# Sixteen short loads on SyncE and 64 semaphore increments on TensorE in an attention kernel

## The chip, the cores and the metric

The kernel runs on one core of a Trainium2 chip. The metric is the device time of one execution in microseconds (us); the time before is the median of three runs, 634.53 us (634.51 to 634.56). A core has five engines with programs of their own: TensorE (PE, matmuls), VectorE (DVE), ScalarE (ACT), GpSimd (POOL) and SyncE (SP, which here issues loads). They meet through semaphores. Transfers run on 16 DMA engines, which take their work from queues.

## The reference

Attention without a mask, for 8 x 16 = 128 heads, 16 queries and 2048 keys of 256 elements a head, in bf16:

```python
B, H, Sq, Skv, Dh = 8, 16, 16, 2048, 256

def reference(q, k, v):
    scale = q.shape[-1] ** -0.5
    scores = jnp.einsum('bhqd,bhkd->bhqk', q, k) * scale
    attn = _softmax(scores, axis=-1)
    return jnp.einsum('bhqk,bhkd->bhqd', attn, v)
```

K and V are 134 MB each; all of both has to be read once.

## The kernel before

**Tiling.** The 128 heads are worked in G = 16 blocks of 8 heads; 8 heads x 16 queries fill the 128 partitions. A block's K is 8 MB, loaded in two halves of 4 MB (`load_k`, e = 0 and 1), its V is 8 MB. `SL` is the buffer for all of it: four slots of 4 MB, two for V (VA, VB) and two for K (KA, KB). There is one buffer for the K and one for the V of a block, so a load waits until TensorE has read what stood there. Block 0's K goes through the V slots.

**Stages of a block.** VectorE transposes K in place in 32 x 32 blocks (`kt`, L196, four for a block). TensorE makes the scores (`qk`, 64 matmuls into `S_ps`, lines L309 and L310). VectorE takes the maximum (L220), ScalarE the exponential (L292), VectorE transposes the result (L229, L231), and VectorE and ScalarE copy it into the sparse weights `PTz` (L203, L205, L277). TensorE multiplies with V (`pv`, L332, 128 matmuls with a weight load each into `O_ps`), ScalarE scales the output into `O_fin` (L271) and issues the store (L301).

**TensorE's program** (`on_tensor`). It waits for the first query weights (`c_qw`, L337), clears the score banks with four matmuls, computes the scores of block 0 in small loops, and enters the main loop over r = 1 to 16: scores of block r (up to 15), 20 matmuls into `X_ps` that nothing reads in most rounds, then PV of block r - 1. The loop is rolled: each round runs the same instructions, some 64 score matmuls and 128 PV matmuls with their weight loads.

**SP's program** (`on_sync`). It issues every load on one queue (q1 in the profile), in program order, and each load waits for the semaphore that says its slot is free: `c_qk` counts finished score halves, `c_pv` finished sixteenths of PV. After the start, a loop over j = 2 to 14 issues the two halves of K of block j (L146, L127) and then V of block j - 1 (L147, L132, L133). The last K comes in quarters, the last two blocks of V in 3 and 9 pieces (`PIECES`), each with a semaphore of its own, so that PV can start on what has landed. At the end SP waits for the last eviction (`c_ev`, L155), issues the last store (L156) and waits for it.

**GpSimd's program** (`on_gpsimd`) begins with 17 semaphore increments (L163), which set starting counts.

Of the kernel before, what the change touches and what calls it, by code (L numbers as in the profile page):

```python
# [11 lines left out]
BF16 = mybir.dt.bfloat16  # L12
# [8 lines left out]
def bass_standalone__softmax_full_bidir__sampling_kernel(  # L21
# [16 lines left out]
    ku = k.rearrange("b h s d -> (b h s) d").rearrange("(u p t) d -> u p t d", p=128, t=T)  # L38
# [4 lines left out]
    with ExitStack() as es:  # L43
        ec = es.enter_context
# [9 lines left out]
        PTz = ec(nc.sbuf_tensor("PTz", [128, 2, T, 128], BF16))  # L54
        mk = ec(nc.sbuf_tensor("mk", [128, 1], F32))
        O_fin = ec(nc.sbuf_tensor("O_fin", [128, D], BF16))
        negm = ec(nc.sbuf_tensor("negm", [128, 1], F32))
        lsum = ec(nc.sbuf_tensor("lsum", [128, 2], F32))
        ltot = ec(nc.sbuf_tensor("ltot", [128, 1], F32))
# [6 lines left out]
        def sem(name):  # L66
            return ec(nc.semaphore(name))
# [6 lines left out]
        s_v0 = sem("s_v0")  # L74
        s_st = sem("s_st")
        s_fin = sem("s_fin")
        c_pool = sem("c_pool")
        c_qt = sem("c_qt")
        c_cq = sem("c_cq")
# [46 lines left out]
        def load_k(eng, g, e, slot, t0, n, s):  # L126
            eng.dma_start(SL[:, slot, t0:t0 + n, :], ku[2 * g + e, :, t0:t0 + n, :]).then_inc(s, 16)  # L127

        def on_sync(eng):
            def load_v(w, a, n):  # L130

                eng.wait_ge(c_pv, 8 * w + (a + n + C - 1) // C)  # L132
                eng.dma_start(VW[:, a:a + n, :], vb[w, :, a:a + n, :]).then_inc(s_p[w][a] if a else s_v, 16)  # L133

            eng.dma_start(QX, qh).then_inc(s_q, 16)  # L135
            for g, s0, s in ((0, VA, s_k0), (1, KA, s_k)):
                for e in range(2):
                    load_k(eng, g, e, s0 + e, 0, T, s[e])

            for e in range(2):  # L140
                eng.wait_ge(c_qk, 4 * e + 4)
                eng.dma_start(VW[:, T * e:T * e + T, :], vb[0, :, T * e:T * e + T, :]).then_inc(s_v0 if e else s_v, 16)
            with nc.Fori(2, last, engines=[SP]) as j:
                for e in range(2):
                    eng.wait_ge(c_qk, 8 * j + 4 * e - 4)
                    load_k(eng, j, e, KA + e, 0, T, s_k[e])  # L146
                load_v(j - 1, 0, 2 * T)  # L147
            for e in range(2):
                eng.wait_ge(c_qk, 8 * last + 4 * e - 4)
                load_k(eng, last, e, KA + e, 0, T // 2, s_k[e])  # L150
                load_k(eng, last, e, KA + e, T // 2, T // 2, s_kl[e])
            for w in PIECES:
                for a, n in PIECES[w]:
                    load_v(w, a, n)
            eng.wait_ge(c_ev, G + 1)  # L155
            eng.dma_start(oh[last], O_fin[:]).then_inc(s_fin, 16)  # L156
            eng.wait_ge(s_fin, 16)

# [146 lines left out]
        def on_tensor(eng):  # L305
            def mm(dst, w, x, start, stop, load, check=True):

                if load:
                    return eng.matmul(dst, w, x, start=start, stop=stop, skip_group_check=not check)  # L309
                return eng.add_instruction(mybir.InstMatmult(  # L310
                    name=nc.get_next_instruction_name(), engine=PE, start_tensor_calc=start, stop_tensor_calc=stop,
                    bass_skip_group_check=not check, ldweights=False, tile_size=(128, 128), tile_position=(0, 0),
                    ins=[eng.lower_ap(x), eng.lower_ap(w, for_matmul_weights=True)], outs=[eng.lower_ap(dst)]))

            def qk(e, cs, slot):
                for bp in range(8):
                    for c in cs:
                        ins = mm(S_ps[:, c, :], QW[:, e, :, bp], SLk[:, slot, c, bp // 2, bp % 2, :, :],
                                 e == 0 and bp == 0, e == 1 and bp == 7, c == cs[0])
                return ins  # L320

            def pv(lim):

                for t in range(2 * T):
                    if t == T:
                        eng.wait_ge(s_v0, 16)
                        eng.wait_ge(c_cp, 10 * r + 1)
                        eng.wait_ge(c_cd, 6 * r)
                    for w in s_p:
                        if t in s_p[w]:  # L330
                            eng.wait_ge(s_p[w][t], lim[w])
                    ins = eng.matmul(O_ps[:, 0:D], PTz[:, t // T, t % T, :], VW[:, t, :],  # L332
                                     start=(t == 0), stop=(t == 2 * T - 1))
                    if t % C == C - 1:
                        ins.then_inc(c_pv, 1)

            eng.wait_ge(c_qw, 4)  # L337

            for c in range(4):
                if c == 0:  # L340
                    eng.wait_ge(c_pool, 1)
                mm(S_ps[:, c, :], PTz[:, 0, 0, :], PTz[:, 0, 0:4, :].rearrange("p t m -> p (t m)"), True, False, c == 0, False)
            with nc.Fori(0, 2, engines=[PE]) as e:
                for h in range(2):
                    with nc.Fori(0, 4, engines=[PE]) as b:
                        eng.wait_ge(c_kt, 2 * e + h + 1)
                        for par in range(2):
                            for c in (2 * h, 2 * h + 1):
                                ins = mm(S_ps[:, c, :], QW[:, e, :, 2 * b + par], SLk[:, VA + e, c, b, par, :, :],
                                         False, False, c == 2 * h, False)  # L350
                        if h:
                            ins.then_inc(c_qk, 1)

            with nc.Fori(1, G + 1, engines=[PE]) as r:
                rr = eng.to_reg(r)
                with eng.If_lt(rr, G):
                    for e in range(2):
                        for h in range(2):
                            eng.wait_ge(c_kt, 4 * r + 2 * e + h + 1)
                            if e + h == 0:  # L360
                                eng.wait_ge(c_ex[1], rr)
                            ins = qk(e, (2 * h, 2 * h + 1), KA + e)
                        ins.then_inc(c_qk, 4)

                    mid = eng.to_reg(((r + 14) & 16) + ((r + 1) & 16))
                    with eng.If_eq(mid, 16):
                        with nc.Fori(0, SPARE, engines=[PE]) as x:
                            for _ in range(4):
                                mm(X_ps[:], QW[:, 1, :, 7], QT[:, 0:512], True, True, False)
                lim = {last - 1: eng.to_reg(((r + 1) & 16) + 1), last: eng.to_reg((r & 16) + 1)}  # L370
                eng.wait_ge(c_ev, rr)
                eng.wait_ge(c_cp, 10 * r - 5)
                eng.wait_ge(c_cd, 6 * r - 2)
                eng.wait_ge(s_v, 16 * r)
                pv(lim)

        on_sync(nc.sync)
        on_gpsimd(nc.gpsimd)
        on_vector(nc.vector)
        on_scalar(nc.scalar)  # L380
        on_tensor(nc.tensor)


# [26 lines left out]
```

## Time and profile before

| | us |
|---|---|
| median of three runs (lowest, highest) | 634.53 (634.51, 634.56) |
| the profiled execution | 634.58 |
| its span in the profile | 633.3 |
| TensorE matmul busy | 539.7 (85%) |
| VectorE busy | 444.2 (70%) |
| ScalarE busy | 241.8 (38%) |
| moved by DMA | 270.56 MB, 427 GB/s over the span |

The profile is of one execution. Its page gives busy times of engines and queues, a chain of work that ended last (followed back from the last instruction, at each step to what released it), and groups of instructions by source line. Names such as SPq or PEldq stand for an engine's own sequencer: register steps, semaphores, issuing of transfers. A DMA queue's row has its packets, MB, and the time of its packets as a share of 16 engines' time in the window. Instruction queues (q8, q14) carry blocks of the engines' programs. A share can come out a little over 1, since a packet is counted where it starts.

### The profile page before, as it was taken

How to read it: one execution, taken by the hardware profiler on the slowest of the kernel's cores; microseconds unless marked ns; L12 is line 12 of the kernel's file. 1: busy time of each engine (PE TensorE's matmuls, PEld its weight loads, DVE VectorE, ACT ScalarE, POOL GpSimd, SP SyncE). 2: the span in 40 equal slices, each digit the busy share in tenths (PEclk: the TensorE clock that was granted, in tenths of full speed). 3: DMA queues.
4: the chain of work that ended last, by engine and by line, in shares of the span. 5: the costliest groups of instructions: out<-in, count | busy, mean ns of one | idle time of the engine just before them, and what ended most of it. 6: DMA issues, size and time to landing. Idle time of an engine off the chain costs nothing.

```text
span 633.3 us, 8100 instructions
## 1 busy us (share of the span) xinstructions
PE 539.7 (85%) x3336; PEld 272.9 (43%) x2561; DVE 444.2 (70%) x285; ACT 241.8 (38%) x309; POOL 21.5 (3%) x18
## 2 busy tenths in 40 slices
PE   1659989889898897989979899797989979899998
PEld 0112824518244282542725336263362724518386
DVE  5989794765948658496575965759567595769750
ACT  1026542623326233352424425244252442623453
POOL 7600000000000000000000000000000000000000
PEclk9998989999898999989999899999998999999999
DMA  8999999999999999999999999999999999999997
GB/s 364 443 447 433 428 464 401 450 409 431 441 422 442 423 433 458 407 457 408 455 417 421 447 423 441 446 410 457 408 456 417 423 441 424 439 418 430 430 426 299
DMA packets 11234, 270.56 MB, mean 427 GB/s; under 512 B 1248, under 2 KB 3424, under 8 KB 3936
## 3 DMA queue, kind: packets, MB, share of 16 engines
q1 hardware_dynamic: 9072, 269.55, 98.8%
q10 hardware_dynamic: 2160, 0.98, 0.5%
q8 instruction: 1, 0.02, 0.0%
q14 instruction: 1, 0.01, 0.0%
HBM read 269.48 MB, written 1.05 MB: 427 GB/s over the span
## 4 chain that ended last, share of the span: by engine, by line
DMA 57%; PE 34%; DVE 5%; issue 3%; SPq 0%; DVEq 0%; ACT 0%
DMA SL<-in_v_dram 49%; PE O_ps L332 32%; DMA SL<-in_k_dram 8%; DVE SL L196 4%; PE S_ps L309 1%; PE S_ps L310 1%; DVE PTb L231 0%; DVE negm L220 0%; DVE PTa L229 0%; DVE PTz L203 0%; DVE PTz L205 0%; SPq L133 0%; SPq L127 0%; ACT O_fin L271 0%; SPq L135 0%
## 5 line engine op out<-in xcount | busy, mean ns | idle before, releaser
L196 DVE STREAM_TRANSPOSE SL<-SL 128x4096 f32<-128x4096 f32 x64 | 282.4, 4433 | 82.0 <-DMA SL<-in_k_dram 81.2
L309 PE MATMUL S_ps<-SL,QW 128*128 128x512 bf16 (+1 forms) x512 | 206.5, 403 | 68.9 <-DVE SL L196 59.1
L332 PEld LDWEIGHTS O_ps<-SL,PTz 128*128 128x128 bf16 x2048 | 198.6, 98 | 103.1 <-DMA SL<-in_v_dram 79.3
L332 PE MATMUL O_ps<-SL,PTz 128*128 128x256 bf16 x2048 | 227.2, 273 | 12.9 <-DMA SL<-in_v_dram 11.5
L310 PE MATMUL S_ps<-SL,QW 128*128 128x512 bf16 (+1 forms) x512 | 204.8, 400 | 0.0
L309 PEld LDWEIGHTS S_ps<-SL,QW 128*128 128x128 bf16 (+1 forms) x512 | 74.3, 145 | 245.1 <-issue 155.3
L263 ACT ACTIVATE QW<-QT 32x256 bf16 x64 | 26.9, 420 | 203.0 <-PE S_ps L310 201.8
L277 ACT ACTIVATE PTz<-PTa 16x1024 bf16<-16x1024 bf16 x32 | 33.8, 1056 | 111.8 <-PE O_ps L332 100.0
L220 DVE TENSOR_REDUCE negm<-S_ps 128x1 f32<-128x2048 f32 x16 | 36.6, 2289 | 55.1 <-PE S_ps L310 55.1
L310 PE MATMUL X_ps<-QT,QW 128*128 128x512 bf16 x260 | 58.2, 379 | 0.0
L277 ACT ACTIVATE PTz<-PTb 16x1024 bf16<-16x1024 bf16 x48 | 50.6, 1055 | 10.9 <-ACT O_fin L271 10.1
L229 DVE STREAM_TRANSPOSE PTa<-P_sb 128x1024 bf16<-128x1024 bf16 x32 | 39.2, 1224 | 21.9 <-ACT P_sb L292 21.9
L277 ACT ACTIVATE PTz<-PTa,mk 32x1024 bf16<-32x1024 bf16 x48 | 54.3, 1130 | 0.0
L231 DVE STREAM_TRANSPOSE PTb<-P_sb 128x1024 bf16<-128x1024 bf16 (+1 forms) x32 | 39.0, 1219 | 0.0
L292 ACT ACTIVATE P_sb<-S_ps,negm 128x1024 bf16<-128x1024 f32 x32 | 35.3, 1109 | 5.9 <-DVE negm L220 5.9
L277 ACT ACTIVATE PTz<-PTb,mk 32x1024 bf16<-32x1024 bf16 x32 | 36.2, 1132 | 0.0
L271 ACT ACTIVATE O_fin<-O_ps,rinv 128x256 bf16<-128x256 f32 x16 | 7.6, 473 | 51.6 <-PE O_ps L332 51.6
L203 DVE TENSOR_SCALAR PTz<-PTb,mk 32x1024 bf16<-32x1024 bf16 x32 | 15.2, 476 | 0.0
L205 DVE COPY PTz<-PTa 16x1024 bf16<-16x1024 bf16 x32 | 13.5, 422 | 1.6 <-PE O_ps L332 0.6
L170 POOL COPY QT<-PTz 32x1024 bf16<-32x1024 bf16 x12 | 14.3, 1192 | 3.0 <-DVE PTz L187 2.3
L205 DVE COPY PTz<-PTb 16x1024 bf16<-16x1024 bf16 x16 | 6.8, 424 | 3.4 <-PE O_ps L332 3.0
L309 PE MATMUL S_ps<-PTz 128*128 128x512 bf16 x1 | 0.6, 609 | 9.7 <-ACT QW L263 9.7
(21 smaller groups left out, 38.8 us busy)
## 6 DMA issues: line engine op xcount, KB each, us to landing
SL<-in_k_dram SPq DMA_DIRECT2D x30, 4096.0 KB, 24.3
SL<-in_v_dram SPq DMA_DIRECT2D x2, 4096.0 KB, 21.9
SL<-in_k_dram SPq DMA_DIRECT2D x4, 2048.0 KB, 21.1
SL<-in_v_dram SPq DMA_DIRECT2D x1, 3584.0 KB, 21.0
SL<-in_v_dram SPq DMA_DIRECT2D x1, 2560.0 KB, 23.6
SL<-in_v_dram SPq DMA_DIRECT2D x1, 2048.0 KB, 25.0
SL<-in_v_dram SPq DMA_DIRECT2D x1, 1920.0 KB, 11.3
SL<-in_v_dram SPq DMA_DIRECT2D x1, 1600.0 KB, 11.7
```

Of the source, the lines that this page charges most:

```text
L196: eng.transpose(x, x).then_inc(c_kt, 1)
L203: ins = eng.tensor_scalar(out=dst, in0=src, scalar1=m, scalar2=None, op0=ALU.mult)
L205: ins = eng.tensor_copy(dst, src)
L220: eng.tensor_reduce(out=negm[:], in_=S_ps[:].rearrange("p c n -> p (c n)"), axis=AX.X, op=ALU.max, negate=True).then_inc(c_mx, 1)
L229: eng.transpose(fa[:, 1024 * h:1024 * h + 1024], P_sb[:, 16 + 1024 * h:16 + 1024 * h + 1024]).then_inc(c_pt, 1)
L231: eng.transpose(fb[:, 1024 * h:1024 * h + n], P_sb[:, 1024 * h:1024 * h + n]).then_inc(c_pt, 1)
L263: eng.activation(dv, src(a), ACTF.Copy, scale=scale).then_inc(c_qw, 1)
L277: eng.activation(dst, src, ACTF.Copy, scale=m if x else 1.0).then_inc(c_cp, 1)
L292: eng.activation(P_sb[:, 16 + 1024 * h:16 + 1024 * h + 1024], sv, ACTF.Exp, bias=negm[:], scale=1.0, accum_out=lsum[:, h:h + 1]).then_inc( ...
L309: return eng.matmul(dst, w, x, start=start, stop=stop, skip_group_check=not check)
L310: return eng.add_instruction(mybir.InstMatmult(name=nc.get_next_instruction_name(), engine=PE, start_tensor_calc=start, stop_tensor_calc=stop,
L332: ins = eng.matmul(O_ps[:, 0:D], PTz[:, t // T, t % T, :], VW[:, t, :], start=(t == 0), stop=(t == 2 * T - 1))
```

## The change

It adds, and removes nothing.

- A buffer `JK` of 16 partitions, which nothing reads, and two semaphores, `s_jk` and `s_id`.
- In SP's loop, after the two K loads and ahead of the V load, a comparison of j with 5. In that round alone SP issues 16 loads of n = 1 to 16 rows from the start of K (row n of each at the start of partition n's stretch, 32 KB apart), 64 + 8n elements (144 to 384 bytes) a row, into neighbouring columns of `JK`.
- Ahead of the last store, a wait for these 16 loads (`s_jk` at 16 x 16 = 256).
- At the start of TensorE's program, before its first wait, 64 increments of `s_id`, which nothing waits for.

```diff
+        JK = ec(nc.sbuf_tensor("JK", [16, 2112], BF16))
...
+        s_jk = sem("s_jk")
+        s_id = sem("s_id")
...
                     load_k(eng, j, e, KA + e, 0, T, s_k[e])
+
+                jj = eng.to_reg(j)
+                with eng.If_eq(jj, 5):
+                    at = 0
+                    for n in range(1, 17):
+                        w = 64 + 8 * n
+                        eng.dma_start(JK[0:n, at:at + w], ku[0, 0:n, 0, 0:w]).then_inc(s_jk, 16)
+                        at += w
                 load_v(j - 1, 0, 2 * T)
...
             eng.wait_ge(c_ev, G + 1)
+            eng.wait_ge(s_jk, 256)
             eng.dma_start(oh[last], O_fin[:]).then_inc(s_fin, 16)
...
+            for _ in range(64):
+                eng.sem_inc(s_id, 1)
             eng.wait_ge(c_qw, 4)
```

On SP the loop body grows by a comparison, 16 loads and a jump; on TensorE 64 instructions stand ahead of all others. The other engines' programs have the same instructions as before.

## The prediction

> **What bounds the kernel now.** I read the page first: how full the transfer queues are, and the chain that ended last.
>
> ```profile
> span 633.3 us, 8100 instructions
> DMA  8999999999999999999999999999999999999997
> q1 hardware_dynamic: 9072, 269.55, 98.8%
> q10 hardware_dynamic: 2160, 0.98, 0.5%
> q8 instruction: 1, 0.02, 0.0%
> q14 instruction: 1, 0.01, 0.0%
> DMA 57%; PE 34%; DVE 5%; issue 3%; SPq 0%; DVEq 0%; ACT 0%
> ```
>
> The loads that SP issues (q1) keep the 16 DMA engines busy for 98.8% of the span. No compute engine comes near that (TensorE stands at 85% in the page). The transfers themselves set the pace, and I then ask whether any stretch has slack. The table by stretches answers it; its last three columns are the granted clock, the DMA share and GB/s.
>
> ```profile
> 1.80:60.00 58.20, 32.54 (x114) 8.31 (x57) 48.81 (x28) 14.04 (x21) 21.33 (x14) 0.94 1.01 432
> 60.00:80.00 20.00, 18.88 (x150) 13.95 (x138) 15.24 (x17) 10.97 (x17) 0.00 (x0) 1.00 0.98 419
> 80.00:560.00 480.00, 420.92 (x2584) 207.76 (x1939) 340.06 (x212) 185.36 (x234) 0.00 (x0) 0.98 1.01 434
> 615.00:628.20 13.20, 12.07 (x103) 9.68 (x103) 0.15 (x1) 6.33 (x7) 0.00 (x0) 1.00 1.00 415
> 628.20:628.70 0.50, 0.45 (x5) 0.41 (x6) 0.00 (x0) 0.00 (x0) 0.00 (x0) 1.00 0.74 275
> 628.70:629.20 0.50, 0.50 (x7) 0.46 (x5) 0.00 (x0) 0.00 (x0) 0.00 (x0) 1.00 0.36 135
> 629.20:629.60 0.40, 0.40 (x6) 0.26 (x5) 0.00 (x0) 0.00 (x0) 0.00 (x0) 1.00 0.20 76
> 629.60:630.10 0.50, 0.50 (x7) 0.37 (x4) 0.00 (x0) 0.00 (x0) 0.00 (x0) 1.00 0.07 25
> 630.10:632.50 2.40, 1.06 (x10) 0.68 (x8) 0.00 (x0) 0.47 (x1) 0.00 (x0) 1.00 0.00 0
> ```
>
> From 1.8 to 628.2 us the share is 1 within the view's rounding: there is no idle time into which more transfer work could go. The end is more telling. The share falls by steps, and at 629.6 to 630.1 us it is 0.07, which is one engine of 16 (1/16 = 0.06). So the engines don't finish together: one is last by about 0.5 us, and the mean engine is done (1-0.74) x 0.5 + (1-0.36) x 0.5 + (1-0.20) x 0.4 + (1-0.07) x 0.5 = 1.24 us before it. A load counts as landed when its last engine has finished, so **the slowest DMA engine sets the end**, and work added to another one is free up to about 0.5 to 1.2 us. The chain in order of time shows how the end hangs on it:
>
> ```profile
> 614.32 13.88 DMA SL<-in_v_dram
> 628.20 0.05 issue
> 628.25 2.93 PE O_ps L332 x25
> 631.20 0.47 ACT O_fin L271
> ```
>
> A V piece lands at 628.2, 25 matmuls follow without a pause, then the eviction (0.47 us) and the last store. A delay of the landing moves all of this.
>
> **Part 1, SP's time for the 16 loads.** They stand between the second K load of round j = 5 and that round's V load. K loads are issued in pairs from round 2 on, so round 5 is the fourth pair.
>
> ```profile
> 1.19 2.10 SPq L127 DMA_DIRECT2D SL<-in_k_dram  x4
> 169.12 8.35 SPq L127 DMA_DIRECT2D SL<-in_k_dram  x2
> 196.45 0.33 SPq L133 DMA_DIRECT2D SL<-in_v_dram  x1
> ```
>
> Four loads in a row took 2.10 us, 0.525 each; 16 take 8.4 us. SP has issued the second K load at 169.12 + 8.35 = 177.47 and would be through at 185.9. The V load waits for TensorE's block before until 196.45, so 10.6 us of cover are left: cost 0. Without that cover the V load would be late by at most 8.4 us, and the K bytes still queued would hide some of it. The added compare and jump in each of the 13 rounds costs tens of ns in the same sort of wait: 0.
>
> **Part 2, the 16 loads on the DMA engines.** 1 + 2 + ... + 16 = 136 rows of 144 to 384 bytes, behind K of block 5 and ahead of V of block 4 in q1. As the engines have no idle time, each packet costs its engine its full duration. Two windows give prices: the last store alone (630.2 to 633.3 us) and the last V piece (629.2 to 630.2 us).
>
> ```profile
> DMA packets 144, 0.07 MB, mean 21 GB/s; under 512 B 16, under 2 KB 144, under 8 KB 144
> q1 hardware_dynamic: 144, 0.07, 7.1%
> DMA packets 30, 0.04 MB, mean 43 GB/s; under 512 B 5, under 2 KB 26, under 8 KB 30
> q1 hardware_dynamic: 30, 0.04, 11.4%
> ```
>
> The store's 128 rows of 512 bytes and its 16 completion packets took 0.071 x 16 x 3.1 us / 144 = 24.5 ns each; the end of the last piece, rows of 1536 bytes read from HBM, 0.114 x 16 x 1.0 us / 30 = 61 ns each. A store shows 16 packets under 512 bytes beside 128 rows, so a transfer's rows are dealt out to the engines and each adds one completion packet. With 136 rows the mean engine gets 8.5 rows and up to as many completions: 17 x 24.5 ns = 0.42 us. Low bound: the slowest engine gets one row, 2 x 24.5 = 0.05 us. A gain is excluded, as nothing is taken away. High bound: it gets a row of every load at the dearer price, 32 x 61 ns = 1.95 us. I take **0.42 us**, by the store's price, since these rows are shorter still.
>
> [...]
>
> **Part 3, the 64 increments.** They run before TensorE's first wait.
>
> ```profile
> PE S_ps L309 <- ACT QW L263: 9.7, 1, 9.7
> 20.10 0.65 PE L309 MATMUL S_ps<-SL,QW 128*128 x1 [8.50 <-DVE SL L196]
> L163 POOLq EVENT_SEMAPHORE  x17: 17/17/17, 0.7 to 2.0; - x17
> L365 PEldq ALU_OP  x5: 32/36/43, 60.8 to 61.2; - x5
> ```
>
> GpSimd's 17 increments start 1.3/16 = 0.08 us apart, and TensorE's register steps 0.4/4 = 0.1 us apart. So 64 of them last 5 to 6.4 us and end near 7 us; TensorE waits for ScalarE's QW until 9.7, and after four zeroing matmuls again 8.5 us for VectorE. Cost 0; were the 9.7 us exceeded, the second wait would still cover it.
>
> **Part 4, what the increments move.** Every later TensorE instruction stands 64 places further on, the loop with it. This touches the two instruction rows of the page. A window from 65.6 to 68 us has both:
>
> ```profile
> q8 instruction: 1, 0.02, 2.8%
> q14 instruction: 1, 0.01, 0.9%
> 64.53 13.99 PE O_ps L332 x128
> ```
>
> A 16 KB block of program was fetched (2.8% x 16 x 2.4 us = 1.07 us of an engine) and one of 8 KB (0.35 us), while TensorE ran its first PV (64.5 to 78.5), code that it had not reached before; no later round fetched anything. On saturated engines such a fetch is a lasting lag of the one that carries it, and is the likeliest maker of the spread at the end. Moving 64 instructions makes this block due a few us earlier, at the same price on the same engine. I take **0**, with bounds from a gain of 0.5 us (the fetch leaves the saturated stretch, the second-last engine sets the end) to one more fetch at 1.24 us, the lag that the spread shows.
>
> **Part 5, the last wait.** SP's last store now waits for the 16 loads, 430 us after they landed; only this store is behind it. It is one more semaphore instruction after the eviction: GpSimd's stand 0.08 us apart. I take **0.08 us** (0.02 to 0.10).
>
> **Sum.** The profiled execution took 634.58 us, its span of 633.3 and 1.28 around it. 634.58 + 0.42 + 0.08 = 635.08. The median of the runs, 634.53, is 0.05 below it, so 635.0 us for the median.
>
> **Rivals.** *One more fetch* (slower). The loop's code is longer than a 16 KB block, and 64 places later its end can fall into a block that was not needed before. From 67 us to the end of the round at 78.5 TensorE has some 220 instructions left by this row (95 in 5 us):
>
> ```profile
> 65.00:70.00 5.00, 5.00 (x48) 4.47 (x47) 3.63 (x3) 3.78 (x8) 0.00 (x0) 1.00 0.97 411
> ```
>
> If the fetched block began at 67 us and holds fewer than 220 + 64 = 284 instructions, a second fetch comes late in that round: 635.0 + 1.24 = 636.3 us. [...] Against it: TensorE shows no gap there (5.00 busy of 5.00), so the block was asked for ahead of need and probably was the one after, which reaches far enough for both kernels. It also has to be carried by the slowest engine. Chance 0.32.
>
> *The loop no longer fits what TensorE holds* (much slower). [...] Against it: the 16 rounds of PV needed one fetch in all, and nothing shows that the room is at its limit. Chance 0.07. [...] No run here shows the limit.
>
> *Each short load holds its engine for a whole round trip* (slower). The first load needed 4.8 us for 1 MB, of which 1.05 MB at 427 GB/s explain 2.5; 16 x 2.3 us would be 37 us, 672 us. Against it: between 626 and 628.3, where the last short pieces and their completions pass, the queue is full without gaps:
>
> ```profile
> q1 hardware_dynamic: 333, 0.91, 100.8%
> PTz<-in_q_dram SPq DMA_DIRECT2D x1, 1024.0 KB, 4.8
> ```
>
> Chance 0.03. *The loads run in every round*, as if the compare failed: 13 x 0.42 = 5.5 us, 640.1 us; chance 0.01. *The fetch leaves the busy stretch*: 635.0 - 0.5 = 634.5 us, chance 0.05.
>
> **How the numbers follow.** The forecast, 635.0 us, has 0.52. About 0.2% (1.27 us) is what a measurement here can tell from no change: below 633.3 is faster, above 635.8 slower. My own case spans 634.5 to 636.6 by the bounds of part 2; the range 634.2 to 637.0 adds the extra fetch and leaves out the far cases. Slower: the extra fetch (most of its 0.32), the far rivals (0.11), and the dear end of part 2; 0.41. Faster needs more than the 0.5 us that the end's spread offers: 0.03. The rest, 0.56, is no change.
>
> **What would show it.** q1 with 136 more rows, each load's landing before SP's V load; the V load of block 4 still at about 196.5; one 16 KB instruction row, a few us before 66. The single engine at the end still there. A second q8 row in the first round, or one in every round, says that a rival holds. Wrong in the sum: a DMA share below 0.98 near 200 us.

## The result, and the profile after

| | before | changed |
|---|---|---|
| median of 18 runs, us | 634.59 | 635.94 |
| lowest and highest, us | 634.42, 634.81 | 635.24, 639.34 |
| ratio, with its 95% interval | | 1.0023 (1.0017 to 1.0030) |
| profiled execution, us (span) | 634.58 (633.3) | 635.24 (633.9) |

The change costs 1.35 us, or 0.23%. The runs of the changed kernel also spread more: 17 of the 18 lie between 635.24 and 636.42, one at 639.34; those of before lie within 0.4 us. The profiled execution happens to be the fastest of the 18, so its trace shows about half of the loss.

The changed kernel's page, queue rows (packets, MB, share of 16 engines' time):

```profile
span 633.9 us, 8129 instructions
q1 hardware_dynamic: 9344, 269.60, 98.9%
q10 hardware_dynamic: 2160, 0.98, 0.5%
q8 instruction: 2, 0.03, 0.0%
q14 instruction: 1, 0.01, 0.0%
```

SP's queue has 9344 - 9072 = 272 packets more: 136 rows and 136 completions, so a load adds a completion only on the engines that carry its rows. And q8 now has **two** 16 KB program blocks instead of one. The next windows (packets, then the queue row) tell when:

```profile
DMA packets 78, 2.05 MB, mean 410 GB/s; under 512 B 15, under 2 KB 15, under 8 KB 15
q8 instruction: 1, 0.02, 1.3%
...
DMA packets 37, 1.20 MB, mean 399 GB/s; under 512 B 0, under 2 KB 0, under 8 KB 0
q8 instruction: 1, 0.02, 2.3%
```

The first pair is the window from 60 to 65 us, the second that from 77 to 80: one block now starts at 61.1 us, 5.8 us earlier than the block of before (66.9), and another one at 77.9, at the end of the same round. No later round fetches any.

SP's issues in round 5 and the increments on TensorE (timeline, and the view of a source line with its durations and its first and last start), and TensorE's first matmuls:

```profile
169.33 8.33 SPq L131 DMA_DIRECT2D SL<-in_k_dram  x2
177.81 5.71 SPq L157 DMA_DIRECT2D JK<-in_k_dram  x16
196.64 0.37 SPq L137 DMA_DIRECT2D SL<-in_v_dram  x1
...
L351 PEldq EVENT_SEMAPHORE  x64: 51/51/51, 0.8 to 10.5; - x64
...
10.73 0.58 PE L322 MATMUL S_ps<-PTz 128*128 128x512 bf16 x1 [10.73 <-ACT QW L276]
20.38 0.64 PE L322 MATMUL S_ps<-SL,QW 128*128 x1 [7.78 <-DVE SL L209]
```

SP is through with the 16 loads at 183.5, 13 us before V's turn, and V is issued at 196.64 (196.45 before). The increments last until 10.5 us, past the 9.7 us of the first wait, and delay the zeroing matmuls by 1 us. Of the second wait 7.78 us are left of 8.50, so the increments delay nothing else.

The chain that ended last, and the stretches at the end (last three columns: clock, DMA share, GB/s):

```profile
615.02 13.82 DMA SL<-in_v_dram
628.83 0.04 issue
628.88 2.96 PE O_ps L345 x25
631.86 0.47 ACT O_fin L284
```

```profile
628.20:628.70 0.50, 0.50 (x6) 0.26 (x3) 0.00 (x0) 0.00 (x0) 0.00 (x0) 1.00 1.03 399
628.70:629.20 0.50, 0.39 (x4) 0.30 (x4) 0.00 (x0) 0.00 (x0) 0.00 (x0) 1.00 0.91 348
629.20:629.60 0.40, 0.40 (x6) 0.35 (x5) 0.00 (x0) 0.00 (x0) 0.00 (x0) 1.00 0.70 268
629.60:630.10 0.50, 0.50 (x7) 0.36 (x6) 0.00 (x0) 0.00 (x0) 0.00 (x0) 1.00 0.51 197
630.10:630.80 0.70, 0.70 (x9) 0.51 (x7) 0.00 (x0) 0.00 (x0) 0.00 (x0) 1.00 0.25 91
```

The end is the same chain, moved by the landing: 628.83 instead of 628.20, 0.63 us. But many engines now end late. At 629.6 to 630.1 half of them still work, where before only one did. So work was lost on most engines, not on the slowest alone. Where it was lost shows in the seven us from 199 to 206, in which the short loads and the first V packets behind them pass. First the kernel before, then the changed one:

```profile
199.00:206.00 7.00, 4.56 (x15) 0.99 (x7) 6.94 (x4) 4.98 (x5) 0.00 (x0) 0.76 1.09 471
```

```profile
199.00:206.00 7.00, 4.56 (x14) 1.07 (x7) 6.94 (x4) 5.18 (x5) 0.00 (x0) 0.76 1.09 416
```

The engines are counted as busy to the same 1.09 in both (a packet is counted where it starts), but 471 GB/s have become 416. Packets were in work and moved less: (471 - 416) x 7 us is 385 KB, 0.9 us of all 16 engines at 430 GB/s. (Runs without many short packets show 459 to 471 in this stretch, so a few GB/s mean nothing.) The trace's single packets say which. A V packet of 64 KB takes 2.42 us. Right behind the short loads, ten of these packets took 0.2 to 1.65 us longer, while the short packets themselves took only 14 to 22 ns for a row and 9 ns for a completion.

First V packets are stretched now and then without any short load: in the trace of before, three at 122 us by 0.51, 1.00 and 1.23 us, and in that of the increments alone one at 200 us by 0.56. One stretched packet proves little. What is new here is that there are ten, and that they lie on the engines with the most short rows.

### The profile page after: what moved, and what is told of

The parts are those of the page before. It is cut to its first block, busy times and chain, and to the rows that moved or that the text cites. A ratio compares the mean times of both kernels' runs of the same rounds, so it can differ in the third digit from the quotient of the medians.

```text
span 633.9 us, 8129 instructions
## 1 busy us (share of the span) xinstructions
PE 539.9 (85%) x3271; PEld 273.3 (43%) x2561; DVE 444.2 (70%) x285; ACT 241.8 (38%) x309; POOL 21.5 (3%) x18
## 3 DMA queue, kind: packets, MB, share of 16 engines
q1 hardware_dynamic: 9344, 269.60, 98.9%
## 4 chain that ended last, share of the span: by engine, by line
DMA 57%; PE 36%; DVE 4%; issue 2%; SPq 0%; ACT 0%; DVEq 0%
DMA SL<-in_v_dram 49%; PE O_ps L345 32%; DMA SL<-in_k_dram 8%; DVE SL L209 3%; PE S_ps L322 2%; PE S_ps L323 2%; DVE negm L233 0%; DVE PTz L216 0%; DVE PTz L218 0%; ACT P_sb L305 0%; SPq L137 0%; SPq L131 0%; ACT O_fin L284 0%; SPq L139 0%; DVEq L231 0%
## 5 line engine op out<-in xcount | busy, mean ns | idle before, releaser
L322 PE MATMUL S_ps<-SL,QW 128*128 128x512 bf16 (+1 forms) x512 | 208.7, 408 | 64.6 <-DVE SL L209 54.9
L323 PE MATMUL S_ps<-SL,QW 128*128 128x512 bf16 (+1 forms) x512 | 207.0, 404 | 0.0
L323 PE MATMUL X_ps<-QT,QW 128*128 128x512 bf16 x195 | 52.7, 379 | 3.5
```

Of the source, the lines that this page charges most:

```text
L323: return eng.add_instruction(mybir.InstMatmult(name=nc.get_next_instruction_name(), engine=PE, start_tensor_calc=start, stop_tensor_calc=stop,
```

## The experiments

Theories to tell apart: the *hole theory* (short packets ahead of V in SP's queue leave the engines without V bytes in flight, so that the first V packets take longer; *hole* is used below for this stretch of a first V packet) and the *fetch theory* (the second program block makes the loss). Ratios are to the kernel before on the same chip.

### The two parts alone

Loads alone, without the increments:

```diff
-            for _ in range(64):
-                eng.sem_inc(s_id, 1)
```

> The 16 loads and the last wait alone, without the 64 increments. Hole theory (the short packets leave the engines without V bytes in flight, so that the first 64 KB V packets behind them take longer): 0.6 to 1.4 us over the kernel before, near the whole of the change, one 16 KB instruction row. Fetch theory (the second program block makes the loss): 0.4 us, the short packets' own time.

Measured: 636.12 us against 634.54, 1.0025 (1.0016 to 1.0035). That is 1.58 us, a little above the hole theory's 1.4 and far above the fetch theory's 0.4.

Increments alone: buffer, loads and last wait of the change left out.

> The 64 increments alone. Hole theory: two 16 KB instruction rows, but each on another DMA engine, so 0 to 0.3 us over the kernel before. Fetch theory: the second block adds to the slowest engine, 0.9 to 1.3 us.

Measured: 634.55 us against 634.54, 1.0000 (0.9991 to 1.0009), with these rows in its page and at its end:

```profile
q8 instruction: 2, 0.03, 0.0%
...
629.20:629.60 0.40, 0.40 (x6) 0.27 (x5) 0.00 (x0) 0.00 (x0) 0.00 (x0) 1.00 0.21 79
629.60:630.10 0.50, 0.50 (x7) 0.36 (x5) 0.00 (x0) 0.00 (x0) 0.00 (x0) 1.00 0.08 31
```

The increments do bring the second block, and it costs nothing: the last engine ends when it did before (0.07 and 25 GB/s at 629.6 to 630.1). The whole loss belongs to the loads: alone they cost 1.58 us, with the increments 1.35, which the intervals do not tell apart. The fetch theory falls.

### More of it, and less

The 16 loads in blocks 5, 8 and 11, no increments:

```diff
-                with eng.If_eq(jj, 5):
+                for at5 in (5, 8, 11):
+                  with eng.If_eq(jj, at5):
+                    if at5 > 5:
+                        eng.wait_ge(s_jk, 256 * (at5 - 5) // 3)
```

> The 16 loads in blocks 5, 8 and 11, no increments. Hole theory: each time a further hole, two to three times what the loads alone cost, 1.5 to 3.5 us over the kernel before. Fetch theory, packets' own time: 3 x 0.42 = 1.3 us.

Measured: 640.37 us against 634.54, 1.0090 (1.0077 to 1.0104): 5.83 us, 3.7 times the loss of one block, and more than the 3.5 us that the hole theory gave.

The profiled execution, with 641.91 us the slowest of the five, shows one way to lose more than three holes. First the PV of before that starts at 454.61 us, then its counterpart here (start, duration), then a stretch behind it:

```profile
454.61 14.16 PE O_ps L332 x128
...
461.36 16.86 PE O_ps L348 x128
...
477.00:479.00 2.00, 2.00 (x17) 1.26 (x12) 1.97 (x2) 0.47 (x1) 0.00 (x0) 1.00 0.12 49
```

V landed late, PV then ran 2.7 us longer (the granted clock was 0.81 from 460 to 478.4 us, against 1.00 in before), SP could issue the next V load only behind it, and the transfer queue ran dry: a DMA share of 0.12 and 49 GB/s. By its packets the mean engine stood idle for 2.4 us here and for 0.8 us after the second block (355 to 358 us). So up to 3 of the 7.3 us that this execution lost are idle engines behind a late V, and not holes. Why the clock fell there is not shown. The longer program of SP also fetched a second 8 KB block, at 577 us. How the 5.83 us of the median divide is not shown.

One load of 16 rows:

```diff
-                    for n in range(1, 17):
+                    for n in (16,):
```

> One load of 16 rows of 384 bytes in block 5 instead of 16 loads, no increments. If the number of short packets in a row makes the hole: 0 to 0.2 us over the kernel before, no first V packet far over 2.4 us. If any short load makes it: as much as the 16 loads alone, 0.6 us or more.

Measured: 634.54 us against 634.54, 1.0000 (0.9991 to 1.0009). The stretch of 199 to 206 us:

```profile
199.00:206.00 7.00, 4.57 (x15) 0.94 (x7) 6.94 (x4) 4.86 (x5) 0.00 (x0) 0.76 1.07 462
```

The excess of the first V packets is gone: none is stretched here. One row and one completion on an engine open no hole. The number matters.

### Rows, completions, engines

All with rows of 264 bytes, in block 5, without increments. 16 loads of 16 rows:

```diff
-                    at = 0
-                    for n in range(1, 17):
-                        w = 64 + 8 * n
-                        eng.dma_start(JK[0:n, at:at + w], ku[0, 0:n, 0, 0:w]).then_inc(s_jk, 16)
-                        at += w
+                    for n in range(16):
+                        eng.dma_start(JK[0:16, 132 * n:132 * n + 132], ku[0, 0:16, n, 0:132]).then_inc(s_jk, 16)
```

> 16 loads of 16 rows of 264 bytes in block 5, no increments: every engine gets 16 rows and 16 completions. If the hole grows with the short packets of an engine, all engines now have the longest row of them: 1.6 to 2.5 us over the kernel before. If unequal rows (1 to 16 by engine) make the loss: 0.5 us, the packets' own time.

Measured: 636.72 us against 634.65, 1.0034 (1.0021 to 1.0046), 2.07 us, within the hole theory's 1.6 to 2.5.

The same 256 rows in one load:

```diff
+                    eng.dma_start(JK[0:16, 0:2112].rearrange("p (n d) -> p n d", d=132), ku[0, 0:16, 0:16, 0:132]).then_inc(s_jk, 16)
```

> One load with the same 256 rows of 264 bytes, so that each engine has 16 rows but one completion. If the number of rows ahead of V makes the hole: as much as 16 loads of 16 rows. If the completions (one for each load and engine) make it: 0 to 0.5 us over the kernel before.

Measured: 635.56 us against 634.65, 1.0013 (1.0004 to 1.0022), 0.91 us, between the two expectations.

16 loads of one row, `JK[0:1, ...]` from `ku[0, 0:1, n, 0:132]`:

> 16 loads of one row of 264 bytes: all short packets on one engine. If the hole is one of the engine that carries the packets, only this engine falls behind, and the time moves by what it then stands behind the slowest: 0 to 1.5 us over the kernel before, with one stretched first V packet. If it is common to all engines (HBM or SP): as much as the 16 loads of 1 to 16 rows, 1.6 us, with many stretched packets.

Measured: 634.99 us against 634.65, 1.0008 (0.9999 to 1.0017); the runs go from 634.53 to 636.30. The median is not told apart from before.

Four loads of 16 rows, `range(4)`:

> 4 loads of 16 rows of 264 bytes. If the hole opens only past some number of short packets: 0 to 0.3 us over the kernel before. If each load adds its part: a quarter of what 16 loads of 16 rows cost, 0.4 to 0.6 us.

Measured: 634.77 us against 634.65, 1.0002 (0.9993 to 1.0011): no loss clear of noise, and not a quarter of 2.07.

The stretch from 199 to 206 us of the first, the second and the fourth of these:

```profile
199.00:206.00 7.00, 4.55 (x16) 1.14 (x8) 6.94 (x4) 5.11 (x5) 0.00 (x0) 0.83 1.07 330
```

```profile
199.00:206.00 7.00, 4.56 (x21) 1.30 (x9) 6.94 (x4) 4.99 (x5) 0.00 (x0) 1.00 1.16 448
```

```profile
199.00:206.00 7.00, 4.56 (x15) 0.97 (x7) 6.94 (x4) 5.08 (x5) 0.00 (x0) 0.80 1.10 459
```

471 GB/s before becomes 330, 448 and 459. The single packets of the traces, as the excess of an engine's first V packet over 2.42 us:

```
short packets on the engine        excess of its first V packet, us
 1 row,  1 completion              none seen
 4 rows, 4 completions             up to 0.24
16 rows, 1 completion              0.62 to 0.94 on 13 engines, 0.10 to 0.26 on the three
                                   that reach the rows last
16 rows, 16 completions            1.4 to 2.4
16 loads of one row                1.79 on the engine with the rows, 0.11 or less on others
```

Both hypotheses of the second run were too simple: rows alone open a hole of about two thirds of a us, and with as many completions between them it is more than twice that. It grows with the number of short packets of an engine. The changed kernel shows the steps in one trace, as its engines carry 1 to 16 rows with as many completions (the third profile of the section on the runs, below):

```
rows on the engine   1 to 5   6      7      8      9      10     11     12     13     14     15     16
excess, us           0 to .02 0.10   0.34   0.37   1.00   1.10   1.28   1.29   1.43   1.43   1.78   1.80
```

Up to 12 short packets (6 rows) it is nearly nothing, from 18 (9 rows) on a microsecond and more. The third run shows that the hole belongs to the engine that carries the packets: the one V packet stretched by 1.79 us stands right behind the 16 rows.

### Another queue, and spread out

The same 16 loads issued by ScalarE after its last copy of its round 5:

```diff
                 copies(1, (0, 1, 2))
+                with eng.If_eq(gg, 5):
+                    at = 0
+                    for n in range(1, 17):
...
```

> The same 16 loads, no increments, issued by ScalarE at the end of its round 5, so that they pass through the queue of the stores and not ahead of V in SP's queue. If the hole is a matter of what stands ahead of V in the same queue: 0 to 0.5 us over the kernel before. If short packets on an engine make it in any queue: as much as in SP's queue, 1.6 us.

Measured: 634.97 us against 634.62, 1.0006 (0.9997 to 1.0015). No V packet was stretched by more than 0.26 us from 205 to 320 us, while the loads passed. Its page has

```profile
q10 hardware_dynamic: 2432, 1.03, 0.6%
q14 instruction: 2, 0.02, 0.0%
```

the 272 packets in the stores' queue, and a second 8 KB program block, which the kernel before does not fetch: only ScalarE's program has become longer.

This run changes two things at once. In its trace the 136 rows pass one at a time between the large packets of SP's queue, from 258.9 to 302.3 us, where in SP's own queue they all passed within 2.3 us (199.3 to 201.6). So it does not show whether the other queue matters by itself, or only because it spreads the packets.

The loads on SP's queue, four each in blocks 5 to 8:

```diff
+                for b in range(4):
+                    with eng.If_eq(jj, 5 + b):
+                        for n in range(4 * b + 1, 4 * b + 5):
```

> The same 16 loads on SP's queue, no increments, four each in blocks 5 to 8. Hole past some number of short packets in a row: four loads open hardly any, 0 to 0.6 us over the kernel before. A price for each short load wherever it stands: 1.6 us as in one block.

Measured: 634.86 us against 634.62, 1.0005 (0.9996 to 1.0014). The same packets, in the same queue, cost 0.24 us, not clear of noise, instead of 1.58 when no engine has more than eight of them in a row. Two first V packets of block 8 were stretched, by 0.38 and 1.04 us, as single ones are in other traces.

### Why the runs differ

The rows of the loads have 16 different lengths and can be followed packet by packet, so each engine can be told by its number of short rows. The engine numbers in the next expectation are mine and go by these rows: 0 is the engine with 16 of them, 15 the one with a single row, so that 11, 12 and 15 are those with 5, 4 and 1. Two further profiles of the changed kernel as it is:

> The changed kernel as it is, a further profile. If the time of a run hangs on which DMA engines carry the program blocks: other engines than 11, 12 (16 KB) and 15 (8 KB) lag before the short loads, and a run whose lagging engine has many short rows (a low number) is slower, up to 1.9 us over the kernel before; one with only high numbers 0.6 to 0.8. If the engines are always the same: the same three, and 1.35 us comes from elsewhere.

> As the run before it, a third profile of the changed kernel: lagging engines and time are to go together in the same way.

Measured: 635.64 and 635.69 us. The engines that matter, from the packets of the three traces (lag behind the first engine where the short rows begin; time of the short packets; excess of the first V packet; us):

```
profile (time)   short rows   lag    short packets   excess   sum
first (635.24)   13           0.83   0.28            1.42     2.53
                 16           0.19   0.33            1.91     2.43   (0.36 of the 1.91 idle)
                 5            2.00   the last engine before the loads
                 4            1.88
                 1            1.04   0.02            0.00     1.06
second (635.64)  13           1.35   0.28            1.36     2.99
                 16           0.21   0.33            1.81     2.35
                 5            1.95   the last engine before the loads
third (635.69)   13           1.32   0.28            1.43     3.03
                 16           0.23   0.33            1.80     2.36
                 5            1.88   the last engine before the loads
```

In all three, the engine with 5 short rows was last before the loads; in the first and the third, where the packets could be followed back to 60 us, it and the one with 4 rows had carried the two 16 KB program blocks. These two have few short packets and hardly fall back further (an excess of 0 to 0.02 us with 1 to 5 rows). After the loads the engine with 13 rows is last. It overtakes by 2.53 - 2.00 = 0.53, 2.99 - 1.95 = 1.04 and 3.03 - 1.88 = 1.15 us, and the three times lie 0.66, 1.06 and 1.11 us over the profiled time before. My expectation that the fetching engines would change with the run failed; what changed is the lag of the engine with 13 rows, and why it does was not found. The runs above 636 us and the one of 639.34 have no profile, and stay open; a queue run dry after a late V, as in the run with three blocks, is a candidate.

## Why the prediction was right or wrong

**The time** lay in the range and the sign of the sum was right, but the change is 1.35 us where 0.5 was forecast, 635.94 lies above the 635.8 from which I called it slower, and "no change" had the largest chance. Point by point:

- *The bound.* Right: the slowest DMA engine sets the end. The increments' second block, which left it where it was, and the three profiles above show it. In the trace of before each of the last loads updates its semaphore 16 times; those of the load that ends the chain come from 626.28 to 627.64 us, the last alone at 628.20, and TensorE goes on at 628.25.
- *Part 1, SP's time: 0.* Right. 5.71 us for the 16 issues instead of 8.4, V issued in its time.
- *Part 2, the loads on the engines: 0.42 us.* **This is the term that was mis-sized**: the loads alone cost 1.58 us. The packets' own time was even priced too high (0.02 to 0.34 us by engine). What was missing is the stretch of the V packets behind them, up to 1.9 us, which is put at nothing in "each packet costs its engine its full duration"; before has no run of short packets ahead of a large load that could show it. The upper bound of 1.95 us, meant for the dearest packets, held the time by luck. The sign that I had named for a wrong sum, a DMA share below 0.98 near 200 us, did not show (1.09): a stretched packet counts as busy, and only the GB/s fell (471 to 416). The mean of 8.5 rows stood for no single engine: the counts form a staircase, 16 rows on one engine down to 1 on another.
- *Part 3, the increments: 0.* Right by its second cover only. They start (10.5 - 0.8)/63 = 0.154 us apart, not 0.1, and so end at 10.5 us and not near 7.
- *Part 4, the moved program, and the rival of one more fetch.* The second block came in the first round, as that rival said, in both kernels with the increments. Its price was wrong: 1.24 us was counted on the engine that was last already, but the block went to another one, whose equal lag runs beside the first: 634.55 against 634.54 us. How many instructions a block holds was not shown before; in the changed kernel's trace the two fetches start 16.8 us apart (61.1 and 77.9) within one round of TensorE (48.3 to 78.8), with 289 of its instructions between them by the trace's records, so the loop's code does seem longer than a block.
- *The loop that no longer fits.* No round after the first fetched anything: the changed kernel's queues from 80 to 633 us are q1 and q10 alone. How much of its program TensorE holds was not shown.
- *Each short load holds its engine for a round trip.* Wrong by size, 37 us. A loss beyond the packets' own time does occur, but once for a whole run of short packets; whether it is a round trip was not tried. The window that I held against it, full queues among the last pieces, has rows of 1.5 KB and more.
- *Part 5, the last wait: 0.08 us.* Not seen: the eviction starts at 631.86, takes 0.47, and the last store follows at 632.36, 0.03 us later, as before.

**Why 1.35 and not 0.5**, in short: the loads put 1.6 to 1.7 us on the engine with 13 short rows (0.28 and 1.36 to 1.43) and up to 2.2 on those with 15 or 16. Of that only what reaches beyond the engine that was last already counts, 0.53 to 1.15 us in the three profiles. With three blocks the engine with many rows can be last already when the next block comes, so that more of each further hole counts, and late V loads let the queue run dry besides; how much each adds was not measured apart.

What the hole is made of was not shown; shown are its place, its size and what it grows with. No version here is faster than the kernel before.

## What to carry to other kernels

In this saturated queue the price of the small transfers was not their bytes (16 loads of 41 KB in all cost 1.58 us): a run of some 18 or more short packets on one engine, ahead of a large load in the same queue, held up that engine's next large packet by 1 to 2.4 us. Spread them out, so that no engine has more than about eight in a row (0.24 us, not clear of noise, instead of 1.58); one load in place of 16 halved the loss (0.91 against 2.07 us). And where the slowest of 16 DMA engines sets the end, ask of each disturbance which engine it falls on: the second program block, some 1.1 us on another engine than the first one's, cost nothing (634.55 against 634.54 us), and of the 1.6 to 1.7 us on the engine with 13 short rows 0.53 to 1.15 counted. A late landing can cost a second time, when the load that waits for it is issued too late to keep the queue full: with three blocks the mean engine stood idle for 2.4 us behind a V that landed late.

## What the runs showed of the hardware

Blocks of program passed through the same DMA engines as the data: while before's 16 KB block was fetched, from 66.90 to 67.96 us, 15 packets of data were under way beside it, and 16 without it, at 70 us. The 16 KB fetch itself took 1.02 to 1.11 us in the traces of before and of the changed kernel, and in before the data packet right behind it 1.71 us instead of 1.21. The engines that carried the blocks fell behind and, with full queues, stayed behind: in the changed kernel the engines with 4 and 5 short rows stood 1.9 to 2.0 us behind the first one, over 120 us after their fetches. Lengthening ScalarE's program by 16 loads brought a further 8 KB block (two in q14 instead of one), and lengthening SP's by 32 more than the change did brought one too.

Packets of two queues alternated on an engine: in the run with the loads on ScalarE's queue, the 136 short rows passed singly between packets of 32 and 64 KB of SP's queue, over 43 us.
